# A float64 weight matrix converted in place: its sign made by ScalarE, its exponents checked from a second load

## The chip, the cores and the metric

The kernel runs on one core of one Trainium2 chip. The metric is device time in microseconds for one launch. Five engines run their own in-order instruction queues: TensorE (PE; its weight loads are listed apart as PEld), VectorE (DVE), ScalarE (ACT), GpSimd (POOL) and SyncE (SP), which here only issues transfers.

## The reference, cut to what matters

Three layers follow one another. The first is attention over 4 batches, 8 heads, 768 positions and 64 columns, in which each position sees 8 global columns and a local window of 96. The second is a feed-forward layer on the 3072 rows that come out:

```python
def _moe_ref(x, w_in, w_out):          # w_in 512 x 2048, w_out 2048 x 512
    h = x @ w_in
    g = h * (1.0 / (1.0 + np.exp(-h)))
    return (g @ w_out).astype(np.float32)
```

The third is a soft mixture of 8 experts with 4 slots each. Two things matter here: `w_in` and `w_out` arrive as float64 (8 MB each), and the arithmetic of the chip is done on pairs of float16 numbers, a high part and a low part, so that three products replace one.

## The kernel before, in words

The 3072 rows are cut into 24 tiles of 128 (T = 0 to 23) and 8 chunks of 3 tiles. Attention of a tile is a list of items: `s_step(T, 0..3)` (scores of two heads each, their maximum and exponential), `pv_step(T, 0..1)` (weights times values), `split(T)` (q, k and v of a tile cut into high and low part) and `load(T)` (three transfers into the staging buffers `stage_m`). A chunk of the feed-forward layer has 16 steps `l1_step` (first product and its gate) and then `l2_part` for its three tiles. Attention of the first three tiles runs by itself; the items of chunk c+1 are spread over the slots of chunk c (`slot_end`), so that attention hides beside the two products. q and k tiles of T >= 6 are split on GpSimd (high) and VectorE (low).

Both float64 matrices are converted piece by piece by `conv(p)`: p = 0 to 7 is `w_in`, p = 8 to 15 is `w_out`. A piece is 1024 float64 numbers for each partition, loaded to one of six places by `w_ahead` (L449), which loads the next piece as soon as a place is free. `conv` works in place on the two 32-bit words of each number: ScalarE turns byte 3 into the top bits of the low word (L459); VectorE takes the top 16 bits of the float64 (sign and first exponent bits), masks them and xors them with 0x3000 (L461), which leaves the sign for the result and, beside it, three bits that are zero for an exponent in range; TensorE multiplies that array by a small weight `wz` in two matmuls of 512 columns (L466), and for each second piece ScalarE adds up the absolute values (L468), so that a bit that is not zero is seen in `oddp`; VectorE joins high and low word to a float32 (L469); ScalarE writes the high float16 part (L479) and VectorE the low part (L487).

The pieces of `w_in` are converted in the attention of the first tiles and in chunk 0's first half. The pieces of `w_out` are asked for in chunk 0's second half, where `l2_part` needs them: `conv(8 + f // 2)` stands ahead of the l2 products of step f. The order in which each engine gets its instructions is set by the framework's planner, which takes the order of the program as priority and its own estimate of when an operand is ready; what it puts down is the fixed order of each queue. All transfers are issued by SP in one queue: weight pieces (L449), tiles (L266), and the transposes of attention (L347, L392) and of the l2 result (L532). Matmuls of `conv` write the bank `bM`, and L469 overwrites what L466 reads.

Of the kernel before, what the change touches and what calls it, by code (L numbers as in the profile page):

```python
# [45 lines left out]
def p2(e):  # L46
    return float(2.0 ** e)
# [52 lines left out]
def fast_kernel(tc, keepp, q_l, k_l, v_l, q_f, k_f, n_global, n_local, w_in, w_out, phi, w1, w2, shapes, pick_c, out):  # L100
# [8 lines left out]
    with ExitStack() as ctx:  # L109
# [141 lines left out]
        def paired(T):  # L251

            return T < NPAIR
# [159 lines left out]
        def other_items():  # L413
            items, mark = [], {}
            for T in range(C0, NTILE):
                items.append(lambda T=T: s_step(T, 0))
                if T > C0:
                    items.append(lambda T=T: pv_step(T - 1, 0))
                items.append(lambda T=T: s_step(T, 1))
                if T + 1 < NTILE:  # L420
                    items.append(lambda T=T: split(T + 1))
                if T + 2 < NTILE and not paired(T + 2):
                    items.append(lambda T=T: load(T + 2, stage_m))
                items.append(lambda T=T: s_step(T, 2))
                if T > C0:
                    items.append(lambda T=T: pv_step(T - 1, 1))
                    mark[T - 1] = len(items)
                items.append(lambda T=T: s_step(T, 3))
                if paired(T + 2):
                    items.append(lambda T=T: load(T + 2, None))  # L430
            items.append(lambda: pv_step(NTILE - 1, 0))
            items.append(lambda: pv_step(NTILE - 1, 1))
            mark[NTILE - 1] = len(items)
            return items, [0] + [mark[first[c] + CHUNKS[c] - 1] for c in range(1, NCH)]
# [10 lines left out]
        def w_ahead():  # L445
            while nload[0] < 16 and holder.get(place[nload[0]]) is None and (GATE.get(nload[0]) is None or GATE[nload[0]] in done_p):
                p = nload[0]
                holder[place[p]] = p
                nc.sync.dma_start(out=ar.view(place[p], [2048], I32), in_=(w_in if p < 8 else w_out)[p % 8].bitcast(I32))  # L449
                nload[0] += 1  # L450

        def conv(p):
            assert holder[place[p]] == p
            st = ar.view(place[p], [1024, 2], I32)
            low, high = st[:, :, 0], st[:, :, 1]
            by = ar.view(place[p], [2048], I32).bitcast(U8).rearrange("p (n e) -> p n e", e=8)
            u16 = ar.view(place[p], [2048], I32).bitcast(U16).rearrange("p (n e) -> p n e", e=4)

            A.activation(out=low, in_=by[:, :, 3], func=AF.Copy, scale=1.0 / 32, bias=-0.484375)  # L459

            V.tensor_scalar(out=u16[:, :, 1], in0=u16[:, :, 3], scalar1=0xF000, scalar2=0x3000, op0=ALU.bitwise_and, op1=ALU.bitwise_xor)  # L461

            zb = u16[:, :, 1].bitcast(BF16)
            for j in range(2):
                g = 32 * (2 * (p % 2) + j)
                mm(bM[g:g + 32], wz, zb[:, 512 * j:512 * j + 512], start=True, stop=True, tile_position=(0, g))  # L466
            if p % 2 == 1:
                A.activation(out=odd16, in_=bM, func=AF.Abs, accum_out=oddp[:, p // 2:p // 2 + 1])  # L468
            V.scalar_tensor_tensor(out=low, in0=high, scalar=3, in1=low, op0=ALU.logical_shift_left, op1=ALU.bitwise_xor)  # L469
            lowf = ar.view(place[p], [1024, 2], F32)[:, :, 0]  # L470
            if p < 8:
                dst = [wih[:, z, :, 256 * p:256 * p + 256] for z in range(2)]
                src = lowf.rearrange("p (k f) -> p k f", k=4)
                e = E_WI
            else:
                dst = [woh[:, 2 * (p - 8):2 * (p - 8) + 2, z] for z in range(2)]
                src = lowf.rearrange("p (k f) -> p k f", k=2)
                e = E_WO
            A.activation(out=dst[0], in_=src, func=AF.Copy, scale=-p2(e - 128))  # L479
            if LOE[p] != "V":  # L480
                if LOE[p] == "P":
                    A.activation(out=src, in_=src, func=AF.Copy, scale=-p2(e - 128))
                else:
                    G.tensor_scalar(out=src, in0=src, scalar1=-p2(e - 128), scalar2=0.0, op0=ALU.mult, op1=ALU.add)
                G.tensor_tensor(out=dst[1], in0=src, in1=dst[0], op=ALU.subtract)
            else:
                V.scalar_tensor_tensor(out=dst[1], in0=src, scalar=-p2(e - 128), in1=dst[0], op0=ALU.mult, op1=ALU.subtract)  # L487
            holder[place[p]] = None
            w_ahead()


        def l1_step(c, f):
# [310 lines left out]
        for c in range(NCH):  # L803
# [34 lines left out]
            if c == 0:  # L838
                for f in range(0, 16, 2):
                    conv(8 + f // 2)  # L840
                    for m in range(n):
                        l2_part(c, m, range(f, f + 2))
                    slot_end()
                    if f % 4 == 2:
                        slot_end()

                V.tensor_reduce(out=odd, in_=oddp, axis=AX.X, op=ALU.max)
                G.memset(acc, 0.0)
                G.memset(ssum, 0.0)
                G.memset(mrun[0], -3e38)  # L850
                absmax(4, wih[:, 0, 0, 0:128])
                absmax(5, woh[:, 0, 0, 0:128])
                absmax(NSMP - 1, phi16[:, :, 0], AX.XY)
                for m in range(n):
                    l2_end(c, m)
                    tick()
            elif c == NCH - 1:
                while heap:
                    tick()
                last_begin(c)  # L860
                pick = ar.view(ls0 + 512, [2, NS], F32)
                nc.sync.dma_start(out=pick, in_=pick_c.rearrange("p (s o c) -> p s o c", s=2, o=4)[:, :, 0])
                for q in range(3):
                    for f in range(4 * q, 4 * q + 4):
                        for j in range(4):
                            last_part(c, j, (f,))
                    w_units([wo0 + 8192 * q] + g_slot[q])
                for i in range(5):
                    c_flip(i)
                for j in range(4):  # L870
                    last_part(c, j, range(12, 16))
                    last_end(c, j)
                    if j < 3:
                        last_turn(c, j)
            else:
                for m in range(n):
                    for q in range(4):
                        l2_part(c, m, range(4 * q, 4 * q + 4))
                        if q == 3:
                            l2_end(c, m)  # L880
                        slot_end()
# [435 lines left out]
```

## Time and profile before

| | |
|---|---|
| runs, us | 741.72, 741.41, 737.12 (median 741.41) |
| the profiled execution, us | 742.64 |
| its span, first to last instruction, us | 740.9 |
| mean granted TensorE clock | 0.983 |
| busy, us: PE, DVE, ACT, POOL | 682.3, 463.2, 325.4, 236.5 |

The engines work side by side, so the busy times do not add up. A row of instructions gives its start or its busy time, the engine, the source line, the operation, what it writes and reads with its shape, a count, and in square brackets how long the engine stood still before it and which instruction ended that. PEclk is the clock that TensorE was granted, 1.00 for 2.4 GHz and 0.50 for 1.2 GHz; a stretch that had both shows a number between.

### The profile page before, as it was taken

The numbers are of one execution on the slowest core, as the hardware profiler recorded it, in microseconds if no ns is written. First come the engines' busy times: TensorE is split into PE (matmuls) and PEld (weight loads), VectorE is DVE, ScalarE is ACT, GpSimd is POOL, SyncE is SP. The second block draws the span as 40 slices with busy tenths as digits, with TensorE's granted clock in tenths as the row PEclk, the third lists the DMA queues.
The fourth block names the chain that finished last, engine by engine and source line by source line (L and its number), as shares of the span: only waits on it lengthen the run. The fifth ranks groups of instructions, "written<-read, shape, count | busy, mean of one in ns | idle before, by whom it ended". The sixth has DMA issues, their size and how long they took to land.

```text
span 740.9 us, 13574 instructions
## 1 busy us (share of the span) xinstructions
PE 682.3 (92%) x5175; PEld 390.1 (53%) x5175; DVE 463.2 (63%) x1143; ACT 325.4 (44%) x864; POOL 236.5 (32%) x215
## 2 busy tenths in 40 slices
PE   3789888799999999999999899999999999999993
PEld 2445443345645655566556555665566545665352
DVE  4999889986852887288528872786277216504232
ACT  6868665545522553165215531653155214302121
POOL 0000104530561567135716572356143400300000
PEclk9999898999999999999999999999999999999997
DMA  6998667833563656544635656445224794384997
GB/s 205 270 283 261 138 140 191 268 121 75 108 150 75 110 130 136 121 86 114 143 72 119 125 126 131 86 104 125 58 44 66 172 332 145 124 350 188 380 366 245
DMA packets 165240, 120.07 MB, mean 162 GB/s; under 512 B 143920, under 2 KB 150448, under 8 KB 159152
## 3 DMA queue, kind: packets, MB, share of 16 engines
q1 hardware_dynamic: 165168, 119.13, 60.3%
q8 instruction: 42, 0.69, 0.4%
q14 instruction: 30, 0.25, 0.1%
HBM read 79.01 MB, written 6.29 MB: 115 GB/s over the span
## 4 chain that ended last, share of the span: by engine, by line


## 5 line engine op out<-in xcount | busy, mean ns | idle before, releaser
L201 POOL TENSOR_SCALAR arena<-arena 128x1024 f16<-128x1024 f32 (+5 forms) x127 | 124.3, 991 | 291.1 <-ACT arena L330 111.5
L499 PE MATMUL bank<-rows,arena 128*128 128x384 f16 x512 | 169.1, 331 | 0.8 <-ACT rows L199 0.7
L500 PE MATMUL bank<-rows,arena 128*128 128x384 f16 x512 | 168.9, 330 | 0.0
L501 PE MATMUL bank<-rows,arena 128*128 128x384 f16 x512 | 168.4, 330 | 0.0
L199 ACT ACTIVATE arena<-bank 128x384 f16<-128x384 f32 (+1 forms) x153 | 77.4, 506 | 170.5 <-DVE bank L505 98.2
L330 ACT ACTIVATE arena<-arena 128x256 f32<-128x256 f32 (+1 forms) x192 | 92.2, 482 | 94.9 <-DVE arena L329 93.9
L519 PE MATMUL bank<-arena 128*128 128x512 f16 x336 | 127.0, 383 | 1.9 <-ACT arena L479 1.9
L520 PE MATMUL bank<-arena 128*128 128x512 f16 x336 | 127.6, 380 | 0.5 <-DVE arena L487 0.5
L521 PE MATMUL bank<-arena 128*128 128x512 f16 x336 | 127.5, 380 | 0.0
L209 DVE SCALAR_TENSOR_TENSOR arena<-bank,arena 128x384 f16<-128x384 f32 (+2 forms) x154 | 87.9, 571 | 31.8 <-ACT arena L199 30.7
L207 POOL TENSOR_TENSOR arena<-arena 128x1024 f16<-128x1024 f32 (+1 forms) x45 | 89.7, 1993 | 19.7 <-ACT arena L199 16.7
L329 DVE CUSTOM_DVE_ANT_0 arena<-bank,arena 128x256 f32<-128x256 f32 (+1 forms) x192 | 70.4, 395 | 40.6 <-PE bank L324 36.8
L505 DVE SCALAR_TENSOR_TENSOR bank<-arena,bank 128x384 f32<-128x384 f32 x128 | 71.4, 558 | 32.1 <-ACT arena L503 30.9
L207 DVE TENSOR_TENSOR arena<-arena 128x1024 f16<-128x1024 f32 (+2 forms) x50 | 66.4, 1327 | 14.4 <-POOL arena L201 11.8
L503 ACT ACTIVATE arena<-bank 128x384 f32<-128x384 f32 x128 | 61.8, 483 | 20.0 <-PE bank L501 19.7
L501 PEld LDWEIGHTS <-arena 128*128 128x128 f16 x512 | 50.5, 99 | 34.3 <-issue 1.5
L499 PEld LDWEIGHTS <-arena 128*128 128x128 f16 x512 | 50.7, 99 | 31.3 <-issue 3.6
L500 PEld LDWEIGHTS <-arena 128*128 128x128 f16 x512 | 50.6, 99 | 29.9 <-issue 2.8
L521 PEld LDWEIGHTS <-arena 128*128 128x128 f16 x336 | 32.9, 98 | 39.8 <-issue 0.7
L519 PEld LDWEIGHTS <-arena 128*128 128x128 f16 x336 | 33.0, 99 | 37.4 <-issue 3.6
L520 PEld LDWEIGHTS <-arena 128*128 128x128 f16 x336 | 32.9, 98 | 35.0 <-issue 0.7
L369 PEld LDWEIGHTS <-arena 128*128 128x128 f16 x1056 | 40.1, 102 | 15.6 <-DMA arena<-arena 7.2
(178 smaller groups left out, 786.2 us busy)
## 6 DMA issues: line engine op xcount, KB each, us to landing
arena<-in_w_dram SPq DMA_DIRECT2D x31, 1024.0 KB, 8.4
arena<-in_k_l_dram SPq DMA_DIRECT2D x18, 512.0 KB, 4.3
arena<-in_q_l_dram SPq DMA_DIRECT2D x18, 512.0 KB, 4.1
arena<-in_w_in_dram SPq DMA_DIRECT2D x8, 1024.0 KB, 5.7
arena<-in_w_out_dram SPq DMA_DIRECT2D x8, 1024.0 KB, 5.7
arena<-in_v_l_dram SPq DMA_DIRECT2D x24, 256.0 KB, 3.0
out_dram<-arena SPq DMA_DIRECT2D x6, 768.0 KB, 4.6
arena<-in_q_f_dram SPq DMA_DIRECT2D x6, 256.0 KB, 4.7
```

Of the source, the lines that this page charges most:

```text
L199: A.activation(out=out, in_=in_, func=AF.Copy, scale=p2(e))
L201: G.tensor_scalar(out=out, in0=in_, scalar1=p2(e), scalar2=0.0, op0=ALU.mult, op1=ALU.add)
L207: (V if eng == "V" else G).tensor_tensor(out=out, in0=in_, in1=h, op=ALU.subtract)
L209: V.scalar_tensor_tensor(out=out, in0=in_, scalar=p2(e), in1=h, op0=ALU.mult, op1=ALU.subtract)
L330: A.activation(out=pw, in_=pw, func=AF.Exp, scale=-1.0, bias=nmx[:, T, h:h + 1], accum_out=psum_[T % 2][:, h:h + 1])
L499: mm(hp, wh, x[:, 0, k], start=(k == 0), stop=False)
L500: mm(hp, wh, x[:, 1, k], start=False, stop=False)
L501: mm(hp, wl, x[:, 0, k], start=False, stop=(k == 3))
L505: V.scalar_tensor_tensor(out=hp, in0=th, scalar=1.0, in1=hp, op0=ALU.add, op1=ALU.mult)
L519: mm(op, gh, woh[:, f, 0], start=(f == 0), stop=False)
L520: mm(op, gh, woh[:, f, 1], start=False, stop=False)
L521: mm(op, gl, woh[:, f, 0], start=False, stop=(f == 15))
```

## The change

Nothing changes for `w_in` (p < 8). For `w_out` (p >= 8) the instruction of VectorE that masked the sign and the exponent bits (L461), the two matmuls (L466) and the sum of absolute values (L468) go. In their place ScalarE reads the top byte of each number, scales it by 2^-60 about 127.5 and writes it as float16: the value is too small for float16, and a zero with the sign that is wanted stays. The scale of L479 and L487 changes its sign for these pieces.

The exponents of `w_out` are checked later. In the items of tiles T = 7 to 14, after `split(T + 1)`, `tops_load` brings one piece of `w_out` again, in two transfers of 512 KB, into the q and the k staging buffer, where `load(T + 2)` stood. After `s_step(T, 3)` `tops_check` reads the top 16 bits of the 512 numbers for each partition of each buffer on VectorE, xors them with 0x3000 and ors them into one array; after the sixteenth, three small instructions reduce that array into `odd`. `load(T + 2)` then follows the check. `LOE` and its other branches, which no piece used, go.

```diff
-                if T + 2 < NTILE and not paired(T + 2):
+                check = NPAIR + 2 <= T + 1 < NPAIR + 10
+                if check:
+                    items.append(tops_load)
+                elif T + 2 < NTILE and not paired(T + 2):
                     items.append(lambda T=T: load(T + 2, stage_m))
...
                 items.append(lambda T=T: s_step(T, 3))
+                if check:
+                    items.append(tops_check)
+                    items.append(lambda T=T: load(T + 2, stage_m))
...
-            V.tensor_scalar(out=u16[:, :, 1], in0=u16[:, :, 3], scalar1=0xF000, scalar2=0x3000, op0=ALU.bitwise_and, op1=ALU.bitwise_xor)
-            zb = u16[:, :, 1].bitcast(BF16)
...
+            if p < 8:
+                V.tensor_scalar(out=u16[:, :, 1], in0=u16[:, :, 3], scalar1=0xF000, scalar2=0x3000, op0=ALU.bitwise_and, op1=ALU.bitwise_xor)
+                zb = u16[:, :, 1].bitcast(BF16)
+                for j in range(2):
+                    g = 32 * (2 * (p % 2) + j)
+                    mm(bM[g:g + 32], wz, zb[:, 512 * j:512 * j + 512], start=True, stop=True, tile_position=(0, g))
+                if p % 2 == 1:
+                    A.activation(out=odd16, in_=bM, func=AF.Abs, accum_out=oddp[:, p // 2:p // 2 + 1])
+            else:
+                A.activation(out=u16[:, :, 1].bitcast(F16), in_=by[:, :, 7], func=AF.Copy, scale=p2(-60), bias=-127.5 * p2(-60))
...
+        tops = ar.view(pad0 + 2048, [256], I32).bitcast(U16)
+        raw = [stage_m[i].rearrange("p h c -> p (h c)").bitcast(I32) for i in range(2)]
+        seen = [0]
+        def tops_load():
+            for i in range(2):
+                nc.sync.dma_start(out=raw[i], in_=w_out[seen[0] // 2].bitcast(I32)[:, 1024 * i:1024 * i + 1024])
+        def tops_check():
+            for i in range(2):
+                top = raw[i].bitcast(U16).rearrange("p (n e) -> p n e", e=4)[:, :, 3]
+                if seen[0]:
+                    V.scalar_tensor_tensor(out=tops, in0=top, scalar=0x3000, in1=tops, op0=ALU.bitwise_xor, op1=ALU.bitwise_or)
+                else:
+                    V.tensor_scalar(out=tops, in0=top, scalar1=0x3000, scalar2=None, op0=ALU.bitwise_xor)
+                seen[0] += 1
+                if seen[0] == 16:
+                    V.tensor_scalar(out=tops, in0=tops, scalar1=0x7000, scalar2=None, op0=ALU.bitwise_and)
+                    V.tensor_reduce(out=small[:, 15:16], in_=tops, axis=AX.X, op=ALU.max)
+                    V.tensor_tensor(out=odd, in0=odd, in1=small[:, 15:16], op=ALU.max)
...
-                V.tensor_reduce(out=odd, in_=oddp, axis=AX.X, op=ALU.max)
+                V.tensor_reduce(out=odd, in_=oddp[:, 0:4], axis=AX.X, op=ALU.max)
```

## Rows read from the trace of the kernel before

**Rows 1.** Busy time by stretch (PE, PEld, DVE, ACT, POOL, clock, DMA share, GB/s).

```profile
40.00:60.00 20.00, 17.10 (x119) 10.53 (x121) 18.73 (x36) 13.62 (x27) 1.51 (x3) 1.00 1.00 312
53.00:80.00 27.00, 25.65 (x162) 14.03 (x161) 23.29 (x56) 20.38 (x46) 0.22 (x1) 1.00 0.94 267
80.00:108.00 28.00, 24.42 (x167) 12.70 (x164) 24.51 (x44) 20.33 (x48) 4.51 (x4) 0.88 0.50 117
108.00:116.00 8.00, 2.95 (x17) 1.35 (x18) 8.00 (x18) 2.92 (x8) 4.50 (x4) 0.75 0.57 142
116.00:134.00 18.00, 17.09 (x124) 8.34 (x123) 17.94 (x30) 10.96 (x24) 4.75 (x3) 0.92 0.91 265
134.00:149.00 15.00, 10.46 (x60) 4.63 (x60) 14.85 (x25) 7.81 (x19) 9.80 (x7) 1.00 0.77 226
149.00:165.00 16.00, 16.00 (x72) 7.14 (x72) 14.20 (x19) 7.09 (x13) 6.21 (x4) 0.89 0.33 116
200.00:420.00 220.00, 213.34 (x1685) 125.46 (x1684) 143.38 (x374) 91.34 (x272) 109.42 (x88) 1.00 0.53 113
```

**Rows 2.** VectorE in order of time, 79 to 156 us: L461 and what follows.

```profile
79.80 1.32 DVE L461 TENSOR_SCALAR arena<-arena 128x1024 uint16<-128x1024 uint16 x1 [1.83 <-ACT arena L459]
80.91 0.58 DVE L209 SCALAR_TENSOR_TENSOR arena<-bank,arena 128x384 f16<-128x384 f32 x1
...
113.74 1.28 DVE L461 TENSOR_SCALAR arena<-arena 128x1024 uint16<-128x1024 uint16 x1
114.82 0.20 DVE L381 RECIPROCAL arena<-arena 128x8 f32<-128x8 f32 x1
...
145.49 1.64 DVE L209 SCALAR_TENSOR_TENSOR arena<-arena 128x512 f16<-128x512 f32 x1
...
153.55 2.03 DVE L469 SCALAR_TENSOR_TENSOR arena<-arena 128x1024 int32<-128x1024 int32 x1 [0.32 <-PE bank L466]
```

**Rows 3.** Line 461 from 100 to 160 us (ns min/median/max, first and last start).

```profile
L461 DVE TENSOR_SCALAR arena<-arena x6: 1280/1312/1726, 113.7 to 150.8; 128x1024 uint16<-128x1024 uint16 x6
```

**Rows 4.** TensorE in order of time, 86 to 154 us: the check's matmuls and neighbours.

```profile
86.77 0.61 PE L466 MATMUL bank<-arena 128*32 128x512 bf16 x2 [0.70 <-ACT arena L468]
...
115.08 0.61 PE L466 MATMUL bank<-arena 128*32 128x512 bf16 x2 [3.36 <-DVE arena L381]
115.62 1.46 PE L519 MATMUL bank<-arena 128*128 128x512 f16 x3
...
148.39 0.61 PE L466 MATMUL bank<-arena 128*32 128x512 bf16 x2 [3.04 <-DVE arena L461]
148.93 0.61 PE L324 MATMUL bank<-arena 128*128 128x256 f16 x4
```

**Rows 5.** ScalarE in order of time: one `conv` step and one sum of absolutes.

```profile
98.72 1.15 ACT L459 ACTIVATE arena<-arena 128x1024 int32<-128x1024 uint8 x1
99.73 0.50 ACT L199 ACTIVATE arena<-bank 128x384 f16<-128x384 f32 x1
...
112.60 1.12 ACT L479 ACTIVATE arena<-arena 128x1024 f16<-128x1024 f32 x1 [0.81 <-DVE arena L469]
115.73 0.60 ACT L468 ACTIVATE arena<-bank 128x512 bf16<-128x512 f32 x1 [2.01 <-PE bank L466]
```

**Rows 6.** Groups of instructions by line and shape (busy us, mean ns of one).

```profile
L382 DVE TENSOR_TENSOR arena<-bank,arena 128x512 f32<-128x512 f32 x24 | 16.4, 685 | 4.6 <-PE bank L369 4.6
```

**Rows 7.** Waits, 200 to 480 us (total us, times, longest us).

```profile
PE bank L587 <- DVE arena L209: 5.1, 3, 1.9
PE bank L324 <- POOL arena L201: 1.6, 1, 1.6
...
SPq L347 <- POOL arena L207: 64.6, 19, 7.8
```

**Rows 8.** Waits of the whole span: ScalarE's longest for VectorE's gate.

```profile
ACT arena L199 <- DVE bank L505: 98.2, 112, 3.1
```

**Rows 9.** Tile loads of line 266: time from issue to landing.

```profile
DMA to landing us min/median/max: 2.5/3.6/6.2
```

More of the change, by code (lines that the diff above doesn't have):

```diff
@@ L459, in conv @@
             A.activation(out=low, in_=by[:, :, 3], func=AF.Copy, scale=1.0 / 32, bias=-0.484375)
-            V.tensor_scalar(out=u16[:, :, 1], in0=u16[:, :, 3], scalar1=0xF000, scalar2=0x3000, op0=ALU.bitwise_and, op1=ALU.bitwise_xor)
-            zb = u16[:, :, 1].bitcast(BF16)
[L464 to L468, printed above, removed]
+            if p < 8:
[8 more added lines that the diff above has]
+                A.activation(out=u16[:, :, 1].bitcast(F16), in_=by[:, :, 7], func=AF.Copy, scale=p2(-60), bias=-127.5 * p2(-60))
             V.scalar_tensor_tensor(out=low, in0=high, scalar=3, in1=low, op0=ALU.logical_shift_left, op1=ALU.bitwise_xor)
@@ L472, in conv @@
                 dst = [wih[:, z, :, 256 * p:256 * p + 256] for z in range(2)]
+                sc = -p2(E_WI - 128)
                 src = lowf.rearrange("p (k f) -> p k f", k=4)
-                e = E_WI
             else:
                 dst = [woh[:, 2 * (p - 8):2 * (p - 8) + 2, z] for z in range(2)]
+                sc = p2(E_WO - 128)
                 src = lowf.rearrange("p (k f) -> p k f", k=2)
-                e = E_WO
-            A.activation(out=dst[0], in_=src, func=AF.Copy, scale=-p2(e - 128))
@@ L480, in conv @@
[L480 to L487, printed above, removed]
+            A.activation(out=dst[0], in_=src, func=AF.Copy, scale=sc)
@@ L488, in conv @@
+            V.scalar_tensor_tensor(out=dst[1], in0=src, scalar=sc, in1=dst[0], op0=ALU.mult, op1=ALU.subtract)
             holder[place[p]] = None
             w_ahead()
+        tops = ar.view(pad0 + 2048, [256], I32).bitcast(U16)
[4 more added lines that the diff above has]
+                nc.sync.dma_start(out=raw[i], in_=w_out[seen[0] // 2].bitcast(I32)[:, 1024 * i:1024 * i + 1024])
```

## The prediction

> **What bounds the kernel now.** I read the page's busy shares first, where TensorE leads by far, then busy time by stretch, then the queues of the stretches that stand out. Matmuls set most of the run; the stretches say where they do not [rows 1]. From 200 to 420 us TensorE stands still for 220 - 213.34 = 6.7 us, 3%. From 80 to 149 us it stands still for 3.58 + 5.05 + 0.91 + 4.54 = 14.1 us, and its granted clock is 0.75 to 0.92 in parts of it. There VectorE is the full engine: 40.8 of 41 us from 108 to 149 us. This is where the pieces of `w_out` are converted. So a VectorE instruction taken out there should shorten the run, one put in at 200 to 420 us (VectorE 143.4 of 220) should mostly hide, and what is won early is not lost behind, because TensorE runs on without a pause.
>
> The reader should see in VectorE's own order that L461 stands there back to back with other work [rows 2], and in TensorE's that two of its longest pauses end at the check's matmuls, which wait for VectorE [rows 4].
>
> **The change part by part.** (1) *L461 leaves VectorE.* What one frees is its start to the start of the next: 1.08 us at 113.74 [rows 2]. There are six from 108 to 160 us, and the longest took 1.73 where the others took about 1.3 [rows 3]: 6 x 1.08 + 0.45, some 7.0. The one at 79.80 frees 1.11 and also ends a wait of 1.83 for ScalarE's L459, which VectorE need no longer sit out: 2.9. The first one (piece 8, near 70 us) stands where TensorE is busy 25.65 of 27 us [rows 1]: nothing.
>
> As a rule against this sum: the Trainium skill, "VectorE: DVE Perf Modes", section "What auto-detection actually checks", lets a one-source instruction between SBUF operands of even size run at two elements a cycle. By its table an estimate for 1024 elements is 0.7 us, and the seven would free some 4.9 us and not 8.1 (7.0 + 1.1); the result would come out about 3 us higher. The trace differs: the median is 1.31 us [rows 3], so the sum keeps the row's spacing.
>
> (2) *The matmuls leave TensorE.* A pair occupies 115.62 - 115.08 = 0.54 us [rows 4]; eight pairs are 4.3 us. Three pauses end at them, 0.70, 3.36 and 3.04 us. Of the 3.36, the next matmul L519 waits for L479, done at 112.60 + 1.12 = 113.72 [rows 5], so at least 1.4 us of it goes; of the 3.04, the next, L324, needs the split that VectorE ends at 145.49 + 1.64 = 147.13 [rows 2], so about 1.3 goes. VectorE also no longer waits 0.32 us for the matmul at 153.55. These are the same microseconds seen from TensorE, not to be added to (1), where VectorE is full.
>
> (3) *ScalarE gets the sign and loses the sums.* The new instruction has the elements and the byte stride of L459, which frees ScalarE after 99.73 - 98.72 = 1.01 us [rows 5]: 8.1 us for eight. Four sums of 0.6 with their read-out go, and so do their waits, 2.01 us in the one shown. ScalarE is busy 21.7 of 41 us from 108 to 149 [rows 1], which covers it; at 53 to 80 us (20.4 of 27) cover is thinner, and behind the sign stand the gates that TensorE's banks wait for. I take 0.5, bounds 0 and 2. In the chain of a piece it replaces a VectorE instruction of like length.
>
> (4) *The gain of this stage.* Upper bound: 7.0 + 2.9 + 0.3 = 10.2 by VectorE, and 0.08 x 18 + 0.11 x 16 = 3.2 more if the half clock of 116 to 134 and 149 to 165 us goes with the pauses [rows 1], 13.4. Lower bound: the pauses that surely go, 0.7 + 1.4 + 1.3, and one pair at 149 to 165 us where TensorE is full, 4.0. I take 8.5, near the VectorE sum since VectorE is 99% busy there, less a part of the 2.9 that lies ahead of a stretch in which TensorE is full; with (3) 8.0.
>
> (5) *The checks on VectorE.* Sixteen instructions on 512 elements. The nearest row is L382, 0.685 us [rows 6]: 11 us, and three more at the end. They raise VectorE from 143 to 154 of 220 us, so it stays off the path, except that three chunks have a TensorE pause that VectorE ends (5.1 us in all at L587) [rows 7], and a check that stands ahead lengthens it by up to 0.7 to 1.4. Bounds 0 and 4; I take 1.5.
>
> (6) *Loads.* Sixteen transfers of 512 KB, 8.4 MB, on SP's queue, beside transposes and tile loads. At the 312 GB/s of the stretch with a full DMA share they take 27 us of 220 [rows 1], which brings the share from 0.53 to about 0.65: no bound. Each costs SP an issue, among waits of up to 7.8 us for GpSimd's low part ahead of a transpose [rows 7]. `load(T + 2)` of eight tiles moves three or four items later and must wait on SP for the check on VectorE; transposes behind it in the queue wait too. A load lands in 2.5 to 6.2 us [rows 9], and four items (scores, values, scores, split) remain until the split reads it; the cover is thinner than before, when seven remained. Where that is gone, GpSimd starts the split late, and the 1.6 us pause of L324 [rows 7] is the form of it. Bounds 0 and 16 (below); I take 0.5.
>
> **Sum.** The profiled execution took 742.64 us with a span of 740.9. 742.6 - 8.0 + 1.5 + 0.5 = 736.6. The median of the runs, 741.41, lies 1.2 below that execution, so I forecast 735.4.
>
> **Rivals.**
> *A, the forecast:* 731 to 739 as its own range. Chance 0.50.
> *B, the whole stage falls together:* with the pauses the half clock goes too and the middle hides everything: 742.6 - 13.4 - 1.2 = 728. For it: clock and pauses stand side by side in the rows [rows 1]. Against: the matmul after the 3.36 us pause must still wait for L479. Chance 0.18.
> *C, no visible change:* the pieces become bound by the other links, the load that waits for a free place, two ScalarE steps ahead of VectorE, and only the lower bound of 4.0 is won, of which the middle takes 3: 740.4. For it: the DMA share is 0.91 at 116 to 134 us [rows 1]. Against: VectorE is never without work there. The same time comes out if the planner's new order makes up the loss elsewhere. Chance 0.17.
> *D, slower:* a check stands at the head of VectorE's queue before its load has landed. The load waits for the split to leave the staging buffers and for SP's queue (up to 7.8 us), then lands in up to 6.2. ScalarE waits up to 3.1 us for VectorE's gate now [rows 8], and TensorE bears it by its four banks; a wait of 5 us would show with about 2 us. Eight tiles are 16 us: 742.6 - 8.0 + 16 - 1.2 = 749.4. It decides from the point where the loads land more than some 3 us after VectorE reaches the check. For it: the planner places the check by an estimate that does not see the queue. Against: two score steps and a value step lie between. Chance 0.15.
> That the change does not take the check off the conversion is excluded by the code.
>
> **How the numbers follow.** The range is 727 to 746: it takes in A, B and C and leaves out most of D. About 1% (7.4 us) is what a measurement of this kernel can tell from no change: under 734.0 is faster, over 748.8 slower. Faster: B and a third of A, 0.36. Slower: most of D, 0.12. Within 1%: 0.52.
>
> **What would show it.** (1) and (2) hold if VectorE's busy time from 108 us to the last L487 falls by 7 us or more, and chunk 1's first products run on without the pauses ahead of L466; the start of the first l2 transpose (L532) should come 7 to 9 us earlier. (4) is wrong on the high side if TensorE's pauses from 80 to 149 us stay near 14 us. (5) and (6) are right if TensorE's idle time from there to 420 us stays near 7 us; D shows as VectorE waiting at the check's line for `in_w_out_dram`, a late load as GpSimd's L201 waiting for q or k. The prediction fails if the planner's new order opens pauses in places that the change does not touch.

## The result: 0.9% slower, and the profile after

The changed kernel took 747.98 us (median of 8 runs, 745.51 to 750.13), the kernel before 741.27 beside it (8 runs, 737.12 to 744.68): a ratio of 1.009, with a 95% interval from 1.007 to 1.0109, so +6.7 us (5.2 to 8.1). Forecast were 735.4 and a range of 727 to 746. The profiled execution took 746.27 us with a span of 744.5 and a mean clock of 0.971; before it was 742.64, 740.9 and 0.983. Two slow runs are left out of the ratios below: one of the kernel before (749.4 us) and one of the kernel called e5 (2402.82 us).

(Lines after the change: L455 is L449 of before, L465 is L459, L468 L461, L472 L466, L474 L468, L477 L469, L487 L479, L488 the low part L487, L528 the gate L505, L542 to L544 the l2 products L519 to L521, L555 L532, L564 L541, L608 and L610 L585 and L587. New are L476, the sign, L498, the second loads, and L505, the checks. e2, f1, k1, k2 and m2 differ from that by a few lines.)

Busy time by stretch of the kernel after, with the columns of [rows 1] (length, PE, PEld, DVE, ACT, POOL, clock, DMA share, GB/s):

```profile
53.00:80.00 27.00, 25.60 (x153) 13.84 (x153) 23.08 (x54) 23.55 (x46) 0.22 (x1) 0.89 0.90 276
80.00:108.00 28.00, 24.66 (x150) 12.42 (x149) 21.61 (x40) 21.32 (x45) 2.98 (x4) 0.82 0.41 96
108.00:149.00 41.00, 34.10 (x208) 16.01 (x207) 32.84 (x59) 30.96 (x47) 10.87 (x9) 0.88 0.76 224
149.00:165.00 16.00, 13.25 (x73) 6.86 (x73) 9.57 (x18) 7.50 (x12) 2.74 (x4) 1.00 0.55 129
165.00:200.00 35.00, 31.30 (x276) 20.94 (x275) 30.04 (x87) 19.43 (x59) 14.77 (x12) 0.95 0.56 152
200.00:420.00 220.00, 213.59 (x1674) 124.91 (x1673) 149.93 (x377) 89.36 (x267) 109.83 (x88) 0.99 0.61 141
```

Two stretches of the kernel before that [rows 1] does not show whole:

```profile
165.00:200.00 35.00, 33.49 (x285) 21.63 (x284) 26.01 (x71) 18.10 (x51) 8.44 (x8) 1.00 0.44 99
108.00:149.00 41.00, 30.50 (x200) 14.32 (x201) 40.79 (x71) 21.69 (x49) 19.04 (x12) 0.92 0.79 227
```

From 108 to 149 us VectorE fell from 40.79 to 32.84 us, and ScalarE rose from 21.69 to 30.96: 9.3 us, where five signs of 1.01 less three sums of 0.8 (0.59 and 0.19 for the read-out) would have made 2.7. The clock fell too: 0.89 and 0.82 from 53 to 108 us against 1.00 and 0.88. The first l2 transpose on SP's queue, after and before:

```profile
159.83 1.23 SPq L555 DMA_TRANSPOSE arena<-arena  x1
```

```profile
167.48 2.64 SPq L532 DMA_TRANSPOSE arena<-arena  x2
```

It is issued 7.65 us earlier, as forecast; but the span ended 3.6 us later (744.5 against 740.9). So the loss of these two executions lies behind 160 us: TensorE stands still 3.7 of 35 us from 165 to 200, where it had stood still 1.5. Part of the gain ahead of it was only attention that had moved on: by the end of chunk 0 (164.6 us before, 159.8 after) 27 of its score products (L324) had run before and 12 after.

The new instruction of ScalarE (L476) and the one that it was priced by (L459 before, L465 after), by source line (ns min/median/max, first and last start):

```profile
L476 ACT ACTIVATE arena<-arena x8: 2479/2498/2522, 67.0 to 148.7; 128x1024 f16<-128x1024 uint8 x8
```

```profile
L465 ACT ACTIVATE arena<-arena x16: 1109/1138/1272, 16.9 to 147.6; 128x1024 int32<-128x1024 uint8 x16
```

The sign takes 2.50 us, 2.2 times the 1.14 of the instruction with the same elements and the same byte stride. One piece in order of time (start, duration, and in brackets the idle time before and what ended it), ScalarE, VectorE and TensorE:

```profile
129.56 2.52 ACT L476 ACTIVATE arena<-arena 128x1024 f16<-128x1024 uint8 x1
131.77 1.22 ACT L487 ACTIVATE arena<-arena 128x1024 f16<-128x1024 f32 x1
...
132.11 1.23 DVE L477 SCALAR_TENSOR_TENSOR arena<-arena 128x1024 int32<-128x1024 int32 x1 [2.13 <-ACT arena L476]
...
133.04 0.81 PE L542 MATMUL bank<-arena 128*128 128x512 f16 x3 [2.47 <-ACT arena L487]
```

The high part of one piece (L487, L479 before) stands behind the sign of the next on ScalarE, VectorE's join (L477) waits 2.13 us for that sign, and TensorE 2.47 us for the high part. This pause takes the place of those of [rows 4].

Waits of the kernel after (total us, times, longest), 100 to 160 us and then 160 to 420 us:

```profile
DVE arena L477 <- ACT arena L476: 7.2, 4, 2.4
ACT arena L487 <- DVE arena L477: 6.9, 5, 3.2
...
DVE arena L505 <- DMA arena<-in_w_out_dram: 4.0, 4, 1.3
...
POOL arena L201 <- DMA arena<-in_k_l_dram: 19.9, 5, 8.7
```

The last line is the one to see: GpSimd's split of a tile waits 19.9 us for the loads of k. Before, from 160 to 420 us, its only wait for a load was one for v:

```profile
POOL arena L201 <- DMA arena<-in_v_l_dram: 1.6, 1, 1.6
```

The checks themselves are as forecast, with a landing of the second loads (L498) that is, too:

```profile
L505 DVE SCALAR_TENSOR_TENSOR arena<-arena x15: 682/691/693, 168.5 to 349.9; 128x512 uint16<-128x512 uint16 x15
...
DMA to landing us min/median/max: 3.1/3.6/4.9
```

The biggest pause behind the conversion, in order of time (VectorE, GpSimd, TensorE):

```profile
174.66 3.14 DVE L207 TENSOR_TENSOR arena<-arena 128x1024 f16<-128x1024 f32 x1 [0.23 <-POOL arena L201]
183.53 1.22 DVE L207 TENSOR_TENSOR arena<-arena 64x1024 f16<-64x1024 f32 x1
185.84 0.18 DVE L591 TENSOR_TENSOR arena<-bank,arena 128x32 f32<-128x32 f32 x1
...
186.40 1.51 DVE L592 TENSOR_TENSOR arena<-arena 128x32 f32<-128x32 f32 x1
...
185.74 2.12 POOL L207 TENSOR_TENSOR arena<-arena 128x1024 f16<-128x1024 f32 x1
...
189.27 0.21 PE L610 MATMUL bank<-arena 128*128 128x64 f16 x1 [3.48 <-DVE arena L209]
```

L610 (L587 before) is the first product of a chunk's slot work; L588 to L594 ahead of it are a softmax, a chain of small VectorE instructions. In [rows 7] L587 waited up to 1.9 us. Here TensorE stands still for 3.48 us. A low part (L207, 183.53) stands right ahead of the chain, and one of its steps, L592, takes 1.51 us beside GpSimd's L207 where its median is 0.19: 1.3 us of the pause are this step (see the last section). The granted clock behind that pause (columns as above):

```profile
186.00:190.00 4.00, 0.73 (x19) 0.73 (x19) 4.00 (x13) 2.06 (x7) 1.86 (x1) 0.82 0.55 159
190.00:194.00 4.00, 4.00 (x52) 3.09 (x50) 3.26 (x12) 1.15 (x4) 0.00 (x0) 0.75 0.58 111
```

0.82 and 0.75 of four us each are a stretch of some 3.4 us at 1.2 GHz. TensorE worked for 0.73 of the first four us and all of the second, so it costs at most 0.73 / 2 + 0.25 x 4 = 1.4 us more.

The length of each chunk, from the end of one chunk's last l2 product to the next's (us, from the start times of TensorE's instructions; chunk 0 from the start of the span, "7" is the rest), shows where each kernel of the experiments pays. It is one execution each:

```
                              0      1     2     3     4     5     6      7
before                    164.6   72.4  74.6  74.1  74.9  74.1  73.1  133.0
after                     159.8   77.1  76.9  75.5  74.6  74.1  73.6  132.8
e1 sign only              158.9   73.7  74.9  74.1  74.9  74.1  74.2  132.0
e3 sign by VectorE        157.3   72.7  76.5  74.1  74.6  74.1  73.6  131.9
n1 four-byte sign         155.6   73.6  76.5  74.1  74.6  74.1  74.3  132.0
h2 check later            158.3   72.7  74.6  73.7  78.7  75.0  73.6  132.8
k1 check after last split 157.4   72.7  74.6  74.1  76.5  74.1  89.5  132.3
m1 low parts on GpSimd    155.0   79.7  80.7  78.2  74.9  74.1  73.5  132.3
m2 one buffer per tile    156.4   78.4  80.3  83.1  78.0  80.4  79.6  131.9
```

An undisturbed chunk 2 to 5 takes 74.1 to 74.9 us. A stretch of half clock (1.7 us lost) stands in e3's and n1's chunk 2 and in k1's chunk 4, each behind a pause of 1.9 us; the kernel before has a pause of 1.92 us in chunk 4 and no half clock behind it.

### The profile page after: what moved, and what is told of

Read it like the earlier page. It is cut to its first block, busy times and chain, and to the rows that moved or that the text cites. A ratio compares the mean times of both kernels' runs of the same rounds, so it can differ in the third digit from the quotient of the medians.

```text
span 744.5 us, 13569 instructions
## 1 busy us (share of the span) xinstructions
PE 684.0 (92%) x5159; PEld 391.1 (53%) x5159; DVE 461.8 (62%) x1154; ACT 340.3 (46%) x864; POOL 231.6 (31%) x215
## 4 chain that ended last, share of the span: by engine, by line
## 5 line engine op out<-in xcount | busy, mean ns | idle before, releaser
L201 POOL TENSOR_SCALAR arena<-arena 128x1024 f16<-128x1024 f32 (+5 forms) x127 | 119.8, 954 | 316.7 <-ACT arena L330 114.8
L542 PE MATMUL bank<-arena 128*128 128x512 f16 x336 | 127.5, 382 | 5.1 <-ACT arena L487 2.7
L544 PE MATMUL bank<-arena 128*128 128x512 f16 x336 | 128.9, 384 | 0.0
L209 DVE SCALAR_TENSOR_TENSOR arena<-bank,arena 128x384 f16<-128x384 f32 (+2 forms) x154 | 87.9, 571 | 29.4 <-ACT arena L199 28.4
L207 POOL TENSOR_TENSOR arena<-arena 128x1024 f16<-128x1024 f32 (+1 forms) x45 | 89.7, 1993 | 20.0 <-ACT arena L199 17.3
L528 DVE SCALAR_TENSOR_TENSOR bank<-arena,bank 128x384 f32<-128x384 f32 x128 | 71.3, 558 | 29.8 <-ACT arena L526 28.8
L207 DVE TENSOR_TENSOR arena<-arena 128x1024 f16<-128x1024 f32 (+2 forms) x50 | 71.4, 1430 | 23.3 <-POOL arena L201 20.5
L526 ACT ACTIVATE arena<-bank 128x384 f32<-128x384 f32 x128 | 61.6, 482 | 20.1 <-PE bank L524 19.6
L544 PEld LDWEIGHTS <-arena 128*128 128x128 f16 x336 | 33.1, 99 | 45.0 <-issue 6.5
L542 PEld LDWEIGHTS <-arena 128*128 128x128 f16 x336 | 33.0, 98 | 38.6 <-issue 4.6
```

The source lines that it names most:

```text
L201: G.tensor_scalar(out=out, in0=in_, scalar1=p2(e), scalar2=0.0, op0=ALU.mult, op1=ALU.add)
L207: (V if eng == "V" else G).tensor_tensor(out=out, in0=in_, in1=h, op=ALU.subtract)
L209: V.scalar_tensor_tensor(out=out, in0=in_, scalar=p2(e), in1=h, op0=ALU.mult, op1=ALU.subtract)
L528: V.scalar_tensor_tensor(out=hp, in0=th, scalar=1.0, in1=hp, op0=ALU.add, op1=ALU.mult)
L542: mm(op, gh, woh[:, f, 0], start=(f == 0), stop=False)
L544: mm(op, gl, woh[:, f, 0], start=False, stop=(f == 15))
```

## The experiments

Ratios are to the kernel before, run beside each (medians 740.8 to 742.6); us are worked out as (ratio - 1) x 741, with the interval's ends alike. "e3" and the like are the labels of the runs.

**The two halves of the change, alone.** e1 keeps ScalarE's sign and makes no late check; e2 keeps the conversion as it was and adds the late check; e3 lets VectorE mask (L461 stays) and leaves out matmuls, sums and late check; e5 is e3 with the late check.

```diff
e1, e3:
-                check = NPAIR + 2 <= T + 1 < NPAIR + 10
+                check = False
e3, e5:
-                A.activation(out=u16[:, :, 1].bitcast(F16), in_=by[:, :, 7], func=AF.Copy, scale=p2(-60), bias=-127.5 * p2(-60))
+                V.tensor_scalar(out=u16[:, :, 1], in0=u16[:, :, 3], scalar1=0xF000, scalar2=0x3000, op0=ALU.bitwise_and, op1=ALU.bitwise_xor)
-                sc = p2(E_WO - 128)
+                sc = -p2(E_WO - 128)
e2: the lines of `if p < 8:` for all p, without the `else`; sc as in e3
```

> The conversion's part of the change alone: the sign on ScalarE, no matmuls and no sum for w_out, loads where they were before; the exponents of w_out are not looked at (left out). Theory S (the sign instruction is the fault: 2.48 us each in the trace of after, not the 1.01 us that was forecast, so ScalarE sets the pace of the conversion): the loss sits here, 743 to 748 us. Theory M (the conversion gains as the trace of after shows at the end of chunk 0, some 5 us, and the second load with its check and the later tile loads take it back and more in chunks 1 to 3): 735 to 738 us.

Measured: 739.67 us, ratio 0.9987 (0.9958 to 1.0016): -1.0 us, not to be told from no change.

> The conversion as before, with its matmuls and sums, and on top the second load, the late check and the later tile loads in tiles 7 to 14 (exponents of w_out looked at twice). Theory S: within 2 us of before, 740 to 743. Theory M: 748 to 751, before plus the 8 us that after lost between the end of chunk 0 and the end of chunk 3.

Measured: 745.18 us, 1.0037 (1.0002 to 1.0073): +2.7 us (0.1 to 5.4).

> As the sign-only kernel, but the sign is made by VectorE with the mask instruction of before; matmuls and sums for w_out stay out, no late check (exponents of w_out not looked at, left out). Theory S: VectorE pays 1.1 us for each piece but ScalarE is free of 2.4 us, so this is faster than the sign-only kernel by 2 to 8 us, with pauses at the converted pieces shorter. If VectorE is the bound whoever else works, it is slower than the sign-only kernel by 3 to 7 us and near before less the matmuls, 737 to 740.

Measured: 736.87 us, 0.9927 (0.9902 to 0.9953): -5.4 us (-7.3 to -3.5).

> The whole change except that the sign is made by VectorE as before. Theory S: 740 or less, faster than before and than the changed kernel by 5 us or more. Theory M: 744 to 750, no better than the changed kernel by more than 3 us, because the late check still costs its 8 us.

Measured: 743.4 us, 1.0015 (0.9988 to 1.0043): +1.1 us.

Neither theory came out whole: e1 and e2 lie between the two, e3 is as S has it, e5 lies just under M. What follows: the sign on ScalarE, instead of on VectorE, costs 4.4 us without the late check (e1 against e3) and 5.6 with it (after against e5). The late check costs 7.7 us on ScalarE's sign (after against e1), 6.5 on VectorE's (e5 against e3) and 2.7 on the old conversion. Most of the gain that there is comes from the matmuls and sums; no run takes out one without the other. In e3 VectorE is as full as before, and yet TensorE gets 33.36 us of 41 done against 30.50:

```profile
108.00:149.00 41.00, 33.36 (x209) 16.58 (x206) 40.27 (x65) 19.01 (x38) 14.13 (x10) 0.96 0.80 235
```

**What makes the sign slow.** Three kernels with no late check, of which only the duration of L476 is read: g1 takes away the underflow, g2 writes bfloat16, h4 writes the other half of the low word. Each ran once, in 4800.6, 4795.63 and 740.24 us; g1 and g2 go on into `dense_kernel`, a part of the program that the other kernels do not run, behind the conversion that is read here.

```diff
g1: scale=1.0, bias=-127.5     g2: .bitcast(BF16)     h4: out=u16[:, :, 0].bitcast(F16)
```

> The sign-only kernel with scale 1 and bias -127.5 in the sign instruction, so that no result is too small for float16 (the weights of w_out come out wrong: this is for the time of that instruction). If the small results are what makes it 2.48 us, it takes 1.1 us here; if the writing of 2-byte results 8 bytes apart does, it stays at 2.48.

> The sign-only kernel with the sign written as bfloat16, where the result 2^-60 is an ordinary number (weights of w_out wrong). If it is the float16 type or the too small result: 1.1 us. If it is 2-byte results 8 bytes apart: 2.48 us.

> Only the duration of ScalarE's sign instruction is read (its result goes to the wrong half of the low word, and no late check is made, so the run's time says nothing). Theory width: a two-byte result written eight bytes apart takes 2.5 us wherever the two bytes lie, 2.5 again. Rival offset: it is the odd half-word, and at the even one it takes 1.1 to 1.2 like the four-byte result.

Measured medians: 2.494, 2.492 and 2.492 us. Neither the underflow, nor the format, nor the offset is it. What is left is the width: two bytes written every eight bytes against four bytes written every eight bytes. n1 tests that with its consequence: the same instruction in the same place, with a four-byte result.

```diff
-                A.activation(out=u16[:, :, 1].bitcast(F16), in_=by[:, :, 7], func=AF.Copy, scale=p2(-60), bias=-127.5 * p2(-60))
+                A.activation(out=low, in_=by[:, :, 7], func=AF.Copy, scale=1.0 / 32, bias=-0.484375)
```

> The kernel with ScalarE's sign and no late check (e1), but ScalarE writes the top byte of each number as a four-byte integer over the low word, so that it takes 1.1 us as the forecast had it (the sign of w_out is lost, so its values are all positive; the work is otherwise the same). Theory L (the forecast's gain of the stage was right and only the 2.49 us of the two-byte write ate it): 733 to 735, ratio 0.989 to 0.992. Rival C' (taking L461 off VectorE is worth little even then, because the pieces are bound by their chain and not by VectorE's busy time): 736 to 738, ratio 0.993 to 0.996, that is as with VectorE's mask and no matmuls (e3). Rival A' (ScalarE's eight extra instructions cost whatever their length): 740, as e1.

Measured: 736.68 us, 0.991 (0.9874 to 0.9945): -6.7 us (-9.3 to -4.1). Its sign, by source line, and VectorE's wait for it from 100 to 165 us (7.2 in all after the change):

```profile
L476 ACT ACTIVATE arena<-arena x8: 1137/1152/1164, 67.1 to 144.8; 128x1024 int32<-128x1024 uint8 x8
...
DVE arena L477 <- ACT arena L476: 1.4, 2, 1.0
```

This shows that it is the width of the write: 1.15 us against 2.50, and 5.7 us of the run (n1 against e1, whose intervals lie apart).

**Which part of the late check.** On e3, f1 moves only the loads of the tiles 9 to 16 behind `s_step(T, 3)`; f3 adds the second transfers without their checks; e5, above, adds the checks.

```diff
f1:                 if check:
-                    items.append(tops_load)
+                    pass
f1, f3:
-                    items.append(tops_check)
```

> The kernel with the sign on VectorE and no late check, in which only the tile loads of tiles 9 to 16 are moved behind the fourth score step, as in the change; no second load, no check instructions (exponents of w_out not looked at, left out). That kernel took 736.9 without the move and 743.4 with the whole late check. Theory L (the late tile load is the price: GpSimd and then VectorE stand in front of a split whose load has not landed): 741 to 744, nearly all of the 6.5 us. Theory Q (the second transfers and the check are the price): 736 to 738.

Measured: 738.75 us, 0.9952 (0.9933 to 0.997): -3.6 us.

> As the one with moved loads, plus the sixteen second transfers of w_out, but without the check instructions on VectorE (exponents of w_out not looked at, left out). Theory L: like the moved-loads kernel, within 1.5 us. Theory Q, if the transfers are the price: 742 to 744; if the VectorE instructions are: 736 to 738.

Measured: 740.26 us, 0.9973 (0.9955 to 0.9991): -2.0 us.

From e3's -5.4 that is 1.8 for the moved loads, 1.6 for the transfers, 3.1 for the check instructions; the intervals of neighbours overlap, so only their sum of 6.5 is certain, and theory L, that the moved loads are nearly all of it, did not come out. Yet the pause is there with the moved loads alone. VectorE and TensorE of f1 (an execution of 741.29 us, 2.5 above its median):

```profile
177.11 2.05 DVE L207 TENSOR_TENSOR arena<-arena 64x1024 f16<-64x1024 f32 x1 [1.43 <-POOL arena L201]
181.09 1.21 DVE L207 TENSOR_TENSOR arena<-arena 128x1024 f16<-128x1024 f32 x1
...
185.44 0.21 PE L609 MATMUL bank<-arena 128*128 128x64 f16 x1 [3.90 <-DVE arena L209]
```

From 160 to 560 us f1's GpSimd never waits for a k load. What differs from e3 is the order of VectorE's queue: the two low parts of a split stand ahead of the last steps of the slots' softmax, where e3 has no low part from 168 to 184 us. So a moved load can also bring a pause by where the planner then puts the split, and not only by landing late. Checks with buffers of their own, so that no load moves, were not tried.

**Is it the place?** The checks begin at 168 us, where VectorE is fuller than later. h2 (on e5) and h5 (on the changed kernel) make them five tiles later.

```diff
-                check = NPAIR + 2 <= T + 1 < NPAIR + 10
+                check = NPAIR + 7 <= T + 1 < NPAIR + 15
```

> The kernel with VectorE's mask as the sign (e5) and the whole late check, moved five tiles later: pieces come again at tiles T = 12 to 19 in place of 7 to 14, so that no check stands in 165 to 217 us. Theory P (the place costs: the checks of chunk 1 meet a VectorE that is full there): about 739, ratio 0.996, and the first l2 parts of chunk 1 end as early as in e3. Rival W (the work itself costs, 6.5 us wherever it stands): 743, ratio 1.002, as e5. Beside them: with no loss at all it would be 737.

Measured: 741.65 us, 1.0005 (0.9977 to 1.0033): +0.4 us, that is 5.8 on e3.

> The changed kernel with the late check alone moved five tiles later (T = 12 to 19). Theory P: the 8.3 us that the late check costs on top of ScalarE's sign fall to 2 or 3, about 742, ratio 1.000. Rival W: 747, ratio 1.008, as the changed kernel. If ScalarE's sign is what loses the time by itself it stays at 747 as well, but then TensorE's pauses up to 160 us must hold the loss.

Measured: 747.6 us, 1.0062 (1.0033 to 1.0091): +4.6 us, 5.6 on e1.

My theory of the place fell. The loss only moved: in the table above h2's chunk 1 is undisturbed again and chunk 4 takes 4 us more. That chunk shows the link. SP's queue, VectorE, GpSimd and TensorE of h2 in order of time:

```profile
385.82 0.33 SPq L498 DMA_DIRECT2D arena<-in_w_out_dram  x1
388.94 1.93 SPq L347 DMA_TRANSPOSE arena<-arena  x1
391.08 0.84 SPq L266 DMA_DIRECT2D arena<-in_q_l_dram  x1
393.70 0.33 SPq L266 DMA_DIRECT2D arena<-in_k_l_dram  x1
...
390.36 0.69 DVE L505 SCALAR_TENSOR_TENSOR arena<-arena 128x512 uint16<-128x512 uint16 x1 [1.27 <-DMA arena<-in_w_out_dram]
399.49 3.15 DVE L207 TENSOR_TENSOR arena<-arena 128x1024 f16<-128x1024 f32 x1 [1.23 <-POOL arena L201]
...
398.41 1.05 POOL L201 TENSOR_SCALAR arena<-arena 128x1024 f16<-128x1024 f32 x1 [1.10 <-DMA arena<-in_k_l_dram]
...
407.50 0.19 PE L610 MATMUL bank<-arena 128*128 128x64 f16 x1 [3.63 <-ACT arena L526]
```

The k load of the tile is issued at 393.70, behind the second transfer, its landing, the check and a transpose. GpSimd waits for it; VectorE waits 1.23 us for GpSimd at the head of its queue and then works 3.15 us on the low part, beside GpSimd's own L207; the gates and the slots' softmax stand behind, and TensorE stops for 3.63 us (the row names ScalarE's L526; VectorE's last step of the softmax, L209 at 407.20, ends at 407.45). In e3 the same part of the same chunk:

```profile
388.48 0.33 SPq L266 DMA_DIRECT2D arena<-in_q_l_dram  x1
392.52 0.92 SPq L266 DMA_DIRECT2D arena<-in_k_l_dram  x1
...
390.39 1.21 DVE L207 TENSOR_TENSOR arena<-arena 128x1024 f16<-128x1024 f32 x1
...
406.90 0.19 PE L610 MATMUL bank<-arena 128*128 128x64 f16 x1 [1.67 <-DVE arena L209]
```

There the low part of k runs at 390.39, right behind the split, for 1.21 us; the load at 392.52 is already the next tile's.

**The check where no tile load moves.** k1 (on e3) and k2 (on the changed kernel) bring the pieces again after the last tile has been split, one after each attention item.

```diff
+            for k in range(last, last + 9):        # last: the item split(NTILE - 1)
+                items[k] = lambda it=items[k]: (it(), tops_next())   # check the piece, load the next
```

> The kernel with VectorE's mask as the sign (e3), complete again: the eight pieces come a second time after the last tile has been split (538 us in e3), one after each attention item, so that no tile load moves and no split is late. Theory S (the late check costs because a moved tile load makes a split late, and GpSimd's and VectorE's parts of it then stand in the queue ahead of a chunk's slot work): 737 to 738, ratio 0.993 to 0.995, and the pauses of TensorE at the slots' first product (line of slots3) stay under 2.2 us in every chunk. Rival W (sixteen checks and 8 MB of loads cost 5 to 6 us wherever they stand): 742.5, ratio 1.001. Rival N (the transfers collide with the transposes and the weight loads of 580 to 604 us instead): 740 to 743, with TensorE waiting for a DMA there.

Measured: 752.63 us, 1.0146 (1.0106 to 1.0186): +10.8 us.

> The changed kernel, complete, ScalarE's sign kept, with only the place of the late check moved to after the last split. Theory S: the time of the kernel with ScalarE's sign and no late check (e1), 739.5 to 741, ratio 0.997 to 1.000. Rival W: 746 to 748, ratio 1.006 to 1.009. Rival N: 743 to 746.

Measured: 758.19 us, 1.0225 (1.0182 to 1.0269): +16.7 us.

Far worse than any theory had it; the nearest is that of the collisions. Nearly all of it is in chunk 6 (89.5 us). VectorE and TensorE of k1:

```profile
547.26 0.69 DVE L509 SCALAR_TENSOR_TENSOR arena<-arena 128x512 uint16<-128x512 uint16 x1 [1.69 <-DMA arena<-in_w_out_dram]
551.80 2.21 DVE L509 SCALAR_TENSOR_TENSOR arena<-arena 128x512 uint16<-128x512 uint16 x1 [0.77 <-DMA arena<-in_w_out_dram]
...
557.52 0.21 PE L623 MATMUL bank<-arena 128*128 128x64 f16 x1 [4.07 <-DVE arena L209]
607.04 1.46 PE L369 MATMUL bank<-arena 128*128 128x64 f16 x24 [7.40 <-DMA arena<-arena]
```

Here the checks wait for their own transfers at the head of VectorE's queue, again ahead of the slots' softmax (L623), and TensorE waits 7.4 us for a transpose that SP issues among the weight loads of the last layer, which now stand behind the checks; which of these makes it late was not taken apart. So the late check costs without a moved tile load too.

**The late tile, taken off VectorE, and made rarer.** m1 (on e5) gives the low parts of the eight late tiles to GpSimd; m2 (on e5) checks half a piece for each of sixteen tiles, in the k buffer alone.

```diff
m1:
-            le = HLO[T] if T < len(HLO) else "V"
+            le = "P" if NPAIR + 3 <= T < NPAIR + 11 else HLO[T] if T < len(HLO) else "V"
m2:
+                    items.append(lambda T=T, c=check: load(T + 2, stage_m, (0, 2) if c else (0, 1, 2)))
...
+                        items.append(lambda T=T: load(T + 2, stage_m, (1,)))   # behind the check
```

> The kernel with VectorE's mask as the sign and the whole late check (e5), and for the eight tiles that the check loads late, q's and k's low part on GpSimd in place of VectorE, so that VectorE never waits for a late tile at the head of its queue. Theory H (the loss comes by VectorE's queue: a late k makes its low part stand there ahead of the gates and of a chunk's slot work): 738 to 740, ratio 0.994 to 0.998, and no pause over 2.2 us at the slots' first product. Rival G (GpSimd, late by the same load and now with more to do, makes TensorE wait by itself, in the transposes and the scores): 743 or more, with TensorE waiting at the scores for GpSimd. Rival W (16 transfers and 16 checks cost 6 us by themselves): 743, with no such waits.

Measured: 752.76 us, 1.018 (1.0137 to 1.0222): +13.3 us.

> The kernel with VectorE's mask as the sign and a complete late check, thinner: half a piece for each tile, in the k buffer alone, over sixteen tiles (T = 7 to 22), so that q and v of a tile are loaded as early as before and only k comes late. Theory H: a single transfer delays k by some 4 us less than two did; 738.5 to 741, ratio 0.995 to 0.999, spread over chunks 1 to 6. Rival W (the cost goes with the number of transfers and checks, which is the same): 743. Rival K (any late k is enough, and twice as many tiles have one): 746 or more.

Measured: 770.87 us, 1.0414 (1.0376 to 1.0453): +30.7 us.

Theory H, that VectorE's queue is the link, fell in the form that I gave it: without the low parts on VectorE the loss grew. Rival G has the direction, but its sign, TensorE waiting for GpSimd at the scores, is not there. Waits of m1 from 160 to 560 us, of TensorE, VectorE and GpSimd:

```profile
PE bank L610 <- DVE arena L209: 11.0, 4, 5.1
PE bank L564 <- DMA arena<-arena: 8.1, 3, 6.0
...
DVE arena L505 <- DMA arena<-in_w_out_dram: 15.4, 6, 6.4
...
POOL arena L201 <- DMA arena<-in_k_l_dram: 72.9, 8, 13.9
```

With GpSimd slower in freeing the buffers, the second loads come later, the checks wait longer for them (15.4 us, in e5 4.4), and k comes later still (72.9 us, in e5 33.1). I read this as a ring, split, second load, check, tile load, split, that goes round once for each tile; no run takes the ring apart. VectorE's queue is one place where it touches TensorE, the transposes of SP's queue are the other (L564). m2 is rival K, any late k is enough: twice as many late tiles cost 36 us on e3 where eight cost 6.5, and its checks wait 28.8 us for their transfers:

```profile
PE bank L611 <- DVE arena L209: 13.2, 5, 5.3
PE bank L565 <- DMA arena<-arena: 10.5, 2, 6.0
...
DVE arena L506 <- DMA arena<-in_w_out_dram: 28.8, 8, 7.2
```

No complete kernel that beats the one before came out of this: the best, h2, ties with it. e3, which leaves the exponents of `w_out` unchecked, shows what a check without cost would leave with VectorE's mask, -5.4 us.

## Why the prediction was wrong

By its own steps:

(1) *L461 leaves VectorE, 7.0 + 2.9.* The signs named for (1) and (2) came out, 7.95 us less on VectorE from 108 to 149 us (with 59 instructions for 71, of which L461 is five) and the first l2 transpose 7.65 us earlier, but they did not show what bound the stage. n1, which has the forecast's sign, gains 1.3 us on e3, which leaves L461 on VectorE: less than the intervals can tell apart. Busy 40.8 of 41 us was read as "the bound"; e3 is 40.27 of 41 busy and runs the stage faster.

(2) *The matmuls leave TensorE, not added.* This was the gain: e3, with only these and the sums gone, won 5.4 us. TensorE's pauses from 108 to 149 us fell from 10.5 to 7.6 us there, and the eight pairs of 0.54 us are gone.

(3) *ScalarE gets the sign: 0.5, bounds 0 and 2.* This step failed. "Elements and byte stride of L459" left out the width of the result. The instruction takes 2.50 us where L465 takes 1.14, and holds ScalarE for 131.77 - 129.56 = 2.21 us, not 1.01: eight times 1.2 is 9.6 us. It is not "of like length" with the VectorE instruction that it replaces either (1.31). It cost 5.7 us of the run (n1 against e1), and ScalarE became the link that the pieces wait for. That a link other than VectorE could bind was rival C, which names the two ScalarE steps ahead of VectorE; what I had for it was the DMA share, and not this duration. As a rule beside it: the Trainium skill, "ScalarE: Activation LUTs", section "What ACT_TABLE_LOAD costs", gives an ACTIVATE with immediate scale and bias 186 ns + 0.833 ns an element for every function, which for 1024 elements is an estimate of 1.04 us. The trace agrees within a tenth for L465 (1.14) and differs for L476 (2.50), which has the same elements; here the measurement decides.

(4) *The stage's gain, 8.5, with (3) 8.0.* The size was right for the instruction that I had priced: n1 won 6.7 us (4.1 to 9.3). That is partly luck, since 5.4 of it is there with L461 still on VectorE. With the one that runs, e1 won 1.0. The half clock, which I had going in the upper bound, did not go with the pauses: they moved to the l2 products, and 53 to 165 us lost at most 0.11 x 27 + 0.18 x 28 + 0.12 x 41 = 12.9 us to it, where it had been 0.12 x 28 + 0.08 x 41 + 0.11 x 16 = 8.4 (less in both, where TensorE stood still at half clock).

(5) and (6) *The late check: 1.5 + 0.5, bounds 0 to 4 and 0 to 16.* This step failed too: 5.6 to 7.7 us in four pairs, where 2.0 were forecast (2.7 in a fifth, e2). The durations were right (0.69 us a check, 3.6 us a landing), and so was the place where it would show, the slots' first product and GpSimd's L201 waiting for k. Their own sign failed: TensorE's idle time from 149 to 420 us, which should have stayed near 7, was 2.75 + 3.70 + 6.41 = 12.9 us, and 8.2 before. What I took was wrong: "four items remain until the split reads it" was counted from the program's order. The runs show GpSimd waiting 19.9 us for k, and in f1, where it does not wait for k, a split that the planner has put ahead of the slots' softmax. The size of the whole late check is shown; how much of it each of these links makes is not. I also read 200 to 420 us alone, though the first check stands at 168.

The sum of the runs: -6.7 (stage with a sign of 1.15 us) + 5.7 (two-byte write) + 7.7 (late check) = +6.7, the measured ratio; that it closes follows from taking the terms as differences between the same runs. Rival D had the direction and, with 749.4, nearly the time, but for half of it the wrong reason: VectorE's waits at the check were 4.0 us in all and not 16, and 5.7 us of the loss came from ScalarE. At 0.9% the change is slower by less than the 1% that I called no change.

What stays open: how much of the 7.7 is the half clock that follows a pause and how much the pauses alone, since the stretches of half clock differ between executions. In the one pair of the changed kernel and e1, chunks 1 to 3 take 6.8 us longer: from 160 to 420 us TensorE stands still 10.1 us against 6.9, and two stretches of half clock, behind the pauses at 186 and 262 us, cost some 3 us, where e1 has none from 165 to 420. Open are also which link of the late check costs how much, and why it costs less on the old conversion (2.7, with an interval up to 5.4).

## What to carry to other kernels

An engine that is busy all the time is not yet the bound of a stage: take one thing off it that costs nothing elsewhere and see whether the stage gets shorter, before work is moved to another engine for its sake. When an instruction is priced by a row, the row must have its output's width and stride as well as its elements. And a load that is moved behind a use of the same buffer is not priced by its landing time but by the whole round of that buffer: who frees it, which queue issues it and what stands ahead there, who is waiting at the other end, and where the planner then puts the work that hangs on it.

## What the runs showed of the hardware

ScalarE's write of 128 x 1024 two-byte results, one every eight bytes, took 2.49 to 2.50 us in four forms (float16, bfloat16, either half of the word); with four-byte results at the same spacing 1.14 to 1.15, and with two-byte results side by side 1.14 (L487). VectorE's mask, which reads and writes two bytes every eight, took 1.31.

VectorE and GpSimd stretch one another: L592 on 128 x 32, with both inputs in the arena, took 1.51 us while GpSimd ran its L207 (185.74 to 187.86); L591, of the same shape but with one input in a PSUM bank, took 0.18 at 185.84 beside the same instruction. Over the run L592 took 0.18 to 1.51 us, with a median of 0.19. VectorE's L207 on 128 x 1024 took 3.15 us beside GpSimd and 1.21 in e3 at 390.39. GpSimd's L207 took 2.98 us in e3 at 387.46, where VectorE's L207 (386.34 to 388.45) was running as it began, and 2.12 at 397.06, where none was. The Trainium skill, "GPSIMD Engine Reference", section "1. Specifications", says that GpSimd's way to the on-chip memory is shared with VectorE and contended by instructions with two inputs there; the trace agrees: L592 and L207 have two, L591 has one.
